# Sums of products copied out of PSUM by ScalarE, and a new order of work, in a state-space layer with a feed-forward layer behind it

## The chip, the cores and the metric

The kernel runs on one core of one Trainium2 chip. The metric is the device time of one execution in microseconds (us), lower is better. A core has five engines that each work through a queue of their own, strictly in order: TensorE (PE in the profile), VectorE (DVE), ScalarE (ACT), GpSimd (POOL) and SyncE (SP), which here only starts transfers. They wait for one another by semaphores.

## What is computed

The input is a sequence of 2048 rows of 512 values. A conditioning vector gives six modulation vectors. The first half normalizes the rows, modulates them, and convolves each of the 512 columns with its own long kernel K (a state-space model, N = 128 states); the second half normalizes again and applies a feed-forward layer of 1792 hidden values with a squared ReLU.

```
P = exp(dt * A * l),  l = 0..L-1                 # complex, 512 x 128 x 2048
K = real(sum over n of C * P * dt*B)             # 512 x 2048
y = irfft(rfft(u padded) * rfft(K padded))[:L] + u * Dskip
x = x + ga * y(layernorm(x) * (1 + ca) + sa)
h = layernorm(x) * (1 + cb) + sb
x = x + gb * (relu(h @ w1 + b1)**2 @ w2 + b2)
```

## The kernel before

The 512 columns are cut into eight groups c of 64, called A to H. The Fourier transforms are matrix products: for each group, "stage 1" (line 714, four pieces) and "stage 2" (line 724, four pieces) transform the input, the same two stages transform K, VectorE multiplies the spectra (line 864), TensorE sums the products back into the time domain (line 872), and the sums are copied from PSUM into the two large tiles `big0` and `big1` (line 878, in `spread`). The inverse transform of line 1040 reads those tiles; the feed-forward layer follows and fills the second half of the time.

K is made in 32 units u of 16 columns, four to a group. Parameters come first, for groups 0 to 3 and then for 4 to 7: products on GpSimd (lines 518, 532 to 539, 570 to 578), rounding and arc tangent on ScalarE (541 to 569) and VectorE (544 to 575). Then ScalarE makes tables of 24 exponentials (line 801; one group with 64 columns or two with 128). For each unit GpSimd adds a phase (line 810) and multiplies table entries (830 and 834), ScalarE takes sine, absolute value and cosine (820, 821, 822), VectorE multiplies (844 to 847), and TensorE multiplies the two halves (854); ScalarE copies the result out (935).

Ahead of the transforms the sixteen row blocks are normalized. VectorE takes statistics (608, 609), GpSimd turns four variances at a time into 1/sqrt by an addition (612) and a power (613), ScalarE scales a selection matrix (672), VectorE scales the row block (670), TensorE makes the transposed, modulated block (674 and 677), and ScalarE copies it out (680). The blocks are counted #0 to #15 below. The rest of the modulation (lines 634, 698 to 705) is `late_modulation`.

All of stage 1, stage 2, line 677, line 872 and the late modulation share three PSUM banks, `ps0` to `ps2`. A bank is written again only when its former content has been copied out. The convolution's K has a bank pair of its own (`kg`), and sine and cosine another (`tg`).

The order in which the program text emits the steps is set by the string ORDER (one field for each unit; r is a row block, A to H a piece of a group's input transform, a to h a piece of its products and sums, x a table of exponentials, l the late modulation, w and digits loads). It sets which bank each step gets and what depends on what. Which instruction each engine runs next is then chosen by `keep_order`: it plays the program through with the durations of `weight` and takes, for each engine, the ready instruction with the longest way to the end; HURRY adds an amount to that length for some steps. Its choice is fixed in the program, so on the chip an engine waits at an instruction that is not ready, with all behind it.

Of the kernel before, what the change touches and what calls it, by code (L numbers as in the profile page):

```python
# [40 lines left out]
EAGER = (0, 0, 0, 0)  # L41
ON_DVE = {}
PACED = 2
HURRY = (147316, 134417, 27026, 378229, -185473, -185396, -357712, -713)
EXPS = [(0, 1), (1, 1), (2, 2), (4, 2), (6, 2)]
ORDER = (
    "rrrrrrrxrrxrrrrrrrCABCBCBCBCAACB.BBCBAAAAlAC...0aaaa1..aDaaa..DbbbbEE.D2D.DEbbD.xbDDb.EccccccE.F"
    ".EEc3c.F.dddd.EdddFF4.dGFF..eGGeeeF.xGG.GeFHHe5Ge..effffGHf.wHf..HH.6ffwwwHg.g.gH.gww7g.gwgwhhhh"
    "g"
).split(".")  # L50


# [37 lines left out]
def free_size(ap):  # L90
    return math.prod(n for _, n in ap.ap[1:])
# [21 lines left out]
def weight(ins):  # L113
# [3 lines left out]
    if "DMA" in type(ins).__name__:  # L117
# [32 lines left out]
        case "Pool":  # L150
            wide = operands(ins.ins)
            whole = bool(wide) and all(a.ap[-1][0] == 1 and len(a.ap) == 2 for a in wide)
            t = 140 + (2.13 if whole else 1.91 if str(wide[0].bass_ap.dtype) == str(I32) else 1.75) * n if wide else 70 + 1.2 * n
        case _:
            t = 30
# [186 lines left out]
def tile_adaln_ssm_ffn(  # L342
# [18 lines left out]
    nc = tc.nc  # L361
# [79 lines left out]
    z4 = [[f[:, 1024 * c : 1024 * c + 1024].rearrange("p (j d) -> p j d", j=64) for c in range(NC)] for f in flat]  # L441
# [160 lines left out]
    for _ in parameters(0, HEAD):  # L602
        pass
    hurry(mark, HURRY[0])

    mark = len(nc.cur_bb.bb.instructions)
    for s in range(16):
        nc.vector.bn_stats(sts[s % 4], rows[s])
        nc.vector.bn_aggr(mv1[:, s, :], sts[s % 4])
        if s % 4 == 3:  # L610
            var = mv1[:, s - 3 : s + 1, 1]
            nc.gpsimd.tensor_scalar(var, var, EPS, None, op0=ALU.add)
            nc.gpsimd.tensor_tensor(var, var, rsq, op=ALU.pow)
    hurry(mark, HURRY[1])

    for c, n in ((HEAD, NC - HEAD),):
        mark = len(nc.cur_bb.bb.instructions)
        decay(4, 4)
        for _ in parameters(c, n):
            pass  # L620
        hurry(mark, HURRY[2])

# [35 lines left out]
    nc.vector.scalar_tensor_tensor(shift, shift.bitcast(F32), second, s4, op0=ALU.mult, op1=ALU.subtract)  # L658
    hurry(mark, HURRY[3])
    spectra.extend(wms[0:3])  # L660
# [197 lines left out]
    def product_pieces(c):  # L858
        xu, sw, xk = xus[c], sws[c], xks[c]
        yr, yu = spectrum(), spectrum()  # L860
        for g in range(4):
            ps = stage2(xk, g)
            for y, x in ((yr, sw), (yu, xu)):
                nc.vector.tensor_mul(product_piece(y, g), ps, piece(x, g))  # L864
            if g == 3:
                spectra.extend((sw, xu, xk))
            yield

        def sums(ps, g, i, js):
            for h, y in ((0, yu), (1, yr)):  # L870
                for m in range(2):
                    nc.tensor.matmul(  # L872
                        ps[64 * m : 64 * m + 64], pairs(y)[:, g, i // 2, 64 * m : 64 * m + 64, i % 2],
                        e1_sb[:, h].rearrange("p (r j) -> p r j", r=2)[:, :, js], start=(h == 0), stop=(h == 1))

        def spread(ps, js, ds):
            for r in range(2):
                nc.vector.tensor_copy(z4[r][c][:, js, ds], ps.rearrange("p d r j -> p j d r")[..., r])  # L878

        j0 = 0  # L880
        if c == NC - 1:
            j0 = 16
            ps = bank("ps", PS).rearrange("p (d r j) -> p d r j", d=16, r=2)
            for d in range(16):
                sums(ps[:, d], d // 4, d % 4, slice(0, j0))
            spread(ps, slice(0, j0), slice(0, 16))
            yield
        for g in range(4):
            ps = bank("ps", PS).rearrange("p (d x) -> p d x", d=4)[:, :, 0 : 128 - 2 * j0]
            ps = ps.rearrange("p d (r j) -> p d r j", r=2)  # L890
            for i in range(4):
                sums(ps[:, i], g, i, slice(j0, 64))
            spread(ps, slice(j0, 64), slice(4 * g, 4 * g + 4))
            if g == 3:
                spectra.extend((yr, yu))
            yield
# [367 lines left out]
```

## Time and profile before

| | |
|---|---|
| median of 3 runs | 633.45 us (632.07 to 634.69) |
| profiled execution | 632.78 us, span 631.0 us |
| TensorE matmul busy | 588.7 us, 93% of the span |
| VectorE busy | 372.3 us, 59% |
| ScalarE busy | 348.5 us, 55% |
| GpSimd busy | 298.1 us, 47% |
| transfers | 42.32 MB, 67 GB/s on average |

The span is the time from the first to the last instruction of the profiled execution; its own time is 1.78 us longer. Shares are averages over stages that differ: up to 62 us the input is loaded and the rows are prepared, from 62 to about 285 us the transforms run, and from about 320 us on the feed-forward layer.

### The profile page before, as it was taken

What the parts mean: (1) busy time and instruction counts of PE and PEld (TensorE: products, weight loads), DVE (VectorE), ACT (ScalarE), POOL (GpSimd) and SP (SyncE); (2) the same over time, 40 slices, a digit from 0 to 9 for tenths busy, and PEclk for the clock granted to TensorE, in tenths of its full rate; (3) what the DMA queues carried; (4) which work ended last, traced back from release to release, by engine and by line L of the source; (5) the groups of instructions that cost most, each with busy time, mean ns of one, the idle gap of its engine ahead of it and who ended that gap; (6) DMA issues with size and microseconds to landing.
All of it is one profiled execution on the core that took longest, in us unless ns stands there. A gap on an engine that the chain in (4) does not pass through costs nothing.

```text
span 631.0 us, 21224 instructions
## 1 busy us (share of the span) xinstructions
PE 588.7 (93%) x9474; PEld 508.2 (81%) x9474; DVE 372.3 (59%) x652; ACT 348.5 (55%) x651; POOL 298.1 (47%) x247
## 2 busy tenths in 40 slices
PE   1488998999999999998999999999999999999996
PEld 1355988899999999897778888888888888888885
DVE  6888779889688998746556332632326332252224
ACT  4937999979969868543757432253323433222220
POOL 6589799999998998148677300010000100000000
PEclk9979999999999999998999999999999999999999
DMA  8940104131221135465244100100001000010001
GB/s 316 395 146 8 63 12 97 36 70 25 49 50 25 37 82 143 125 187 164 87 137 115 36 1 0 68 0 2 0 1 67 1 1 0 1 66 1 0 1 66
DMA packets 23418, 42.32 MB, mean 67 GB/s; under 512 B 4000, under 2 KB 9504, under 8 KB 23200
## 3 DMA queue, kind: packets, MB, share of 16 engines
q1 hardware_dynamic: 22896, 40.84, 22.0%
q8 instruction: 74, 1.21, 0.8%
q10 hardware_dynamic: 432, 0.14, 0.1%
q14 instruction: 16, 0.13, 0.1%
HBM read 28.39 MB, written 4.19 MB: 52 GB/s over the span
## 4 chain that ended last, share of the span: by engine, by line
PE 75%; ACT 9%; POOL 9%; issue 3%; DVE 3%; DMA 0%; DVEq 0%; POOLq 0%
PE tg L1165 8%; PE tg L1167 8%; PE tg L1166 8%; PE ps L872 7%; PE ps L1131 6%; PE ps L1132 6%; PE ps L1134 6%; PE ps L724 5%; PE ps L714 5%; PE kg L854 3%; PE tg L1040 3%; PE kg L1131 2%; PE kg L1132 2%; PE kg L1134 2%; ACT tables L801 2%
## 5 line engine op out<-in xcount | busy, mean ns | idle before, releaser
L1153 DVE SCALAR_TENSOR_TENSOR ps<-ps,b1c,xy 128x512 f32<-128x512 f32 x42 | 31.8, 756 | 110.7 <-ACT xy L1151 110.7
L1151 ACT ACTIVATE xy<-ps,b1c 128x512 f32<-128x512 f32 x42 | 29.0, 690 | 122.6 <-PE ps L1134 122.6
L1076 POOL TENSOR_TENSOR big<-big,lo 128x512 f32<-128x512 f32 x12 | 15.6, 1300 | 146.9 <-DVE xy L1073 146.5
L724 PE MATMUL ps<-xy,t_sb 128*64 128x64 f32 x2048 | 67.7, 223 | 1.7 <-issue 1.7
L724 PEld LDWEIGHTS ps<-xy,t_sb 128*64 128x64 f32 x2048 | 63.8, 138 | 4.6 <-issue 2.1
L872 PE MATMUL ps<-e_sb,xy 128*64 128x128 f32 (+2 forms) x1152 | 63.6, 266 | 1.9 <-ACT xy L716 1.5
L872 PEld LDWEIGHTS ps<-e_sb,xy 128*64 128x64 f32 x1152 | 58.6, 139 | 3.5 <-ACT xy L716 2.0
L716 ACT COPY xy<-ps 128x512 f32<-128x512 f32 x64 | 36.9, 589 | 13.5 <-PE ps L714 13.4
L834 POOL TENSOR_TENSOR rtl<-tables 128x1024 f32<-128x1024 f32 x22 | 43.3, 1970 | 0.2
L864 DVE TENSOR_TENSOR xy<-ps,xy 128x512 f32<-128x512 f32 x64 | 39.2, 680 | 2.4 <-PE ps L724 1.9
L1131 PE MATMUL ps<-h0h,w1h 128*128 128x512 f32 (+1 forms) x96 | 36.1, 382 | 0.0
L810 POOL TENSOR_TENSOR rtl<-lo,big 128x1024 int32<-128x1024 int32 x16 | 34.3, 2143 | 3.5 <-ACT tg L822 2.8
L810 POOL TENSOR_TENSOR llph<-lo,big 128x1024 int32<-128x1024 int32 x16 | 34.5, 2155 | 1.4 <-ACT tg L822 1.4
L714 PE MATMUL ps<-d_sb,ksb 128*64 128x128 f32 x512 | 34.1, 274 | 0.8 <-DVE xy L864 0.7
L878 DVE COPY big<-ps 128x256 f32<-128x256 f32 (+1 forms) x66 | 24.1, 407 | 17.0 <-PE ps L872 16.9
L714 PE MATMUL ps<-d_sb,big 128*64 128x128 f32 x512 | 32.0, 274 | 1.1 <-ACT big L680 0.7
L1131 PE MATMUL ps<-h,w1h 128*128 128x512 f32 x80 | 31.4, 393 | 0.0
L1153 DVE SCALAR_TENSOR_TENSOR kg<-kg,b1c,xy 128x512 f32<-128x512 f32 x14 | 10.6, 758 | 34.8 <-ACT xy L1151 34.8
L1151 ACT ACTIVATE xy<-kg,b1c 128x512 f32<-128x512 f32 x14 | 9.6, 688 | 37.8 <-PE kg L1134 37.8
L714 PEld LDWEIGHTS ps<-d_sb,ksb 128*64 128x64 f32 x512 | 28.3, 137 | 1.8 <-DVE xy L864 0.9
L714 PEld LDWEIGHTS ps<-d_sb,big 128*64 128x64 f32 x512 | 28.0, 137 | 1.9 <-ACT big L680 1.0
L845 DVE TENSOR_TENSOR rtl<-rtl,tg 128x1024 f32<-128x1024 f32 x22 | 26.6, 1211 | 1.1 <-POOL rtl L834 1.1
(287 smaller groups left out, 1608.3 us busy)
## 6 DMA issues: line engine op xcount, KB each, us to landing
xy<-xt SPq DMA_DIRECT2D x32, 256.0 KB, 4.5
xy<-xy SPq DMA_DIRECT2D x32, 256.0 KB, 3.4
xy<-w_mod SPq DMA_DIRECT2D x6, 1024.0 KB, 8.5
out_dram<-xy SPq DMA_DIRECT2D x16, 256.0 KB, 2.1
xy<-w SPq DMA_DIRECT2D x14, 256.0 KB, 2.7
raw<-w SPq DMA_DIRECT2D x6, 512.0 KB, 4.9
t_sb<-c_t SPq DMA_DIRECT2D x1, 2048.0 KB, 11.0
i2c<-c_i SPq DMA_DIRECT2D x4, 512.0 KB, 4.4
```

Source lines behind the costliest of these rows:

```text
L714: nc.tensor.matmul(ps[64 * r : 64 * r + 64, 128 * i : 128 * i + 128], src[:, i], d1_sb[:, r], start=True, stop=True)
L724: nc.tensor.matmul(ps[64 * r : 64 * r + 64, 64 * i : 64 * i + 64].rearrange("p (h q t) -> p q h t", h=2, t=2), t2_sb[:, 8 * g + i, r], src ...
L810: nc.gpsimd.tensor_tensor(ph.rearrange("p d r (a b) -> p (d r) a b", a=4), bc(low_phase[:, us].rearrange("p d r b -> p (d r) b"), 2, 4), b ...
L834: nc.gpsimd.tensor_mul(am[:, 0, :, 32:96].rearrange("p d (v x) -> p d v x", v=2), bc(et[:, 256 + 8 * d0 : 384 + 8 * d0].rearrange("p (y a) ...
L872: nc.tensor.matmul(ps[64 * m : 64 * m + 64], pairs(y)[:, g, i // 2, 64 * m : 64 * m + 64, i % 2], e1_sb[:, h].rearrange("p (r j) -> p r j" ...
L1131: pe.append(nc.tensor.matmul(ps, w1h[:, q, fs], hh[:, q, cols], start=(q == 0), stop=False))
L1132: pe.append(nc.tensor.matmul(ps, wl[:, q], hh[:, q, cols], start=False, stop=False))
L1134: pe.append(nc.tensor.matmul(ps, w1h[:, q, fs], hl[:, q, cols], start=False, stop=(q == 3)))
L1153: nc.vector.scalar_tensor_tensor(ps, ps, b1c[:, t : t + 1], rr, op0=ALU.add, op1=ALU.mult)
L1165: pe.append(nc.tensor.matmul(acc, r2l[:, ms], hi_, start=(f == 0), stop=False))
L1166: pe.append(nc.tensor.matmul(acc, r2h[:, ms], lo_, start=False, stop=False))
L1167: pe.append(nc.tensor.matmul(acc, r2h[:, ms], hi_, start=False, stop=(f == NF - 1)))
```

## The change

Four things are edited.

- `spread` copies the sums of the products by ScalarE instead of VectorE.
- `weight` gives the power of line 613 (a GpSimd operation on 128 x 4 values with two inputs) 1000 ns; by the general formula it had 147.
- HURRY has eight other numbers.
- ORDER is another string.

```
-HURRY = (147316, 134417, 27026, 378229, -185473, -185396, -357712, -713)
+HURRY = (29580, -181455, -278749, 139035, -280562, -261179, 363664, -461)
 ORDER = (
-    "rrrrrrrxrrxrrrrrrrCABCBCBCBCAACB.BBCBAAAAlAC...0aaaa1..aDaaa..
...
+    "rrrrrrrrrrrrrrrrClABCBCBCCBBAxACB.ABCA.BAAA..C0aaaaa..D.1xaa.a
...
         case "Pool":
             wide = operands(ins.ins)
             whole = bool(wide) and all(a.ap[-1][0] == 1 and len(a.ap) == 2 for a in wide)
+            if len(wide) > 1 and free_size(wide[0]) == 4:
+                return 1000, 1065
...
         def spread(ps, js, ds):
             for r in range(2):
-                nc.vector.tensor_copy(z4[r][c][:, js, ds], ps.rearrange("p d r j -> p j d r")[..., r])
+                nc.scalar.copy(z4[r][c][:, js, ds], ps.rearrange("p d r j -> p j d r")[..., r])
```

Behind line 154 the lines of the changed kernel are two higher (line 613 is its line 615). The order on TensorE from the first matrix product of the inverse transform on is the same in both. Ahead of it, three places matter for what follows. The trailing numbers of names belong to the built program.

The first place is GpSimd's queue from the last parameter product of groups 0 to 3 on (`mv` are the row statistics, `lo` the phases, `tables_379` and `tables_380` the two tables of exponentials, `rtl` and `llph` the tiles of the units). Before:

```order
L572 TENSOR_TENSOR big_83<-big_83 128x4x64
L612 TENSOR_SCALAR mv_71<-mv_71 128x4
L574 TENSOR_TENSOR big_83<-big_83 128x4x128 x3
L613 TENSOR_TENSOR mv_71<-mv_71,small 128x4
L532 TENSOR_TENSOR big_83<-big_83 128x4x64
L533 TENSOR_TENSOR big_83<-big_83 128x4x64
```

The same place now:

```order
L574 TENSOR_TENSOR big_83<-big_83 128x4x64
L806 TENSOR_TENSOR tables_380<-tables_380,big_83 128x64x4 x2
L576 TENSOR_TENSOR big_83<-big_83 128x4x128 x3
L788 TENSOR_TENSOR lo<-lo,big_83 128x128x2 x3
L812 TENSOR_TENSOR rtl<-lo,big_83 128x1024
L806 TENSOR_TENSOR tables_379<-tables_379,big_83 128x64x4
L836 TENSOR_TENSOR rtl<-tables_379 128x16x64
L812 TENSOR_TENSOR llph<-lo,big_83 128x1024
L836 TENSOR_TENSOR rtl<-tables_379 128x16x64
L836 TENSOR_TENSOR llph<-tables_379 128x16x64
L614 TENSOR_SCALAR mv_71<-mv_71 128x4
L615 TENSOR_TENSOR mv_71<-mv_71,small 128x4
```

The power of the last four row blocks, and behind it the parameter products of groups 4 to 7 (now from line 534 on), moved behind the phases and table products of the first units.

The second place is ScalarE's queue among the sixteen row blocks; a copy of line 680 frees the bank of one row block. Before, behind the fifth copy:

```order
L680 COPY big_84<-ps_159 128x128x4
L672 ACTIVATE big_83<-ident,mv_71 128x2x64
L541 ACTIVATE big_83<-big_83,magic 128x4x64
L542 ACTIVATE big_83<-big_83,magic 128x4x64
L550 ACTIVATE big_83<-big_83 128x4x64
L551 ACTIVATE big_83<-big_83 128x4x64
L543 ACTIVATE big_83<-big_83,unmagic 128x4x64
L680 COPY big_84<-ps_157 128x128x4
```

Now, behind the fourth copy (line 682 is the copy, line 822 the first sine):

```order
L682 COPY big_84<-ps_158 128x128x4
L674 ACTIVATE big_83<-ident,mv_71 128x2x64
L822 ACTIVATE tg_425<-rtl 128x1024
L823 ACTIVATE rtl<-rtl 128x1024
L682 COPY big_84<-ps_159 128x128x4
L682 COPY big_84<-ps_157 128x128x4
```

And now, further on, with the copies of #11 to #15 (here with buffer numbers):

```order
L674 ACTIVATE big0_83<-ident_63,mv1_71 128x2x64 x2
L682 COPY big1_84<-ps0_157 128x128x4
L674 ACTIVATE big0_83<-ident_63,mv1_71 128x2x64 x2
L682 COPY big1_84<-ps1_158 128x128x4
L682 COPY big1_84<-ps2_159 128x128x4
L543 ACTIVATE big0_83<-big0_83,magic_64 128x4x64
L544 ACTIVATE big0_83<-big0_83,magic_64 128x4x64
L552 ACTIVATE big0_83<-big0_83 128x4x64
L553 ACTIVATE big0_83<-big0_83 128x4x64
L682 COPY big1_84<-ps0_157 128x128x4
L545 ACTIVATE big0_83<-big0_83,unmagic_65 128x4x64
L682 COPY big1_84<-ps1_158 128x128x4
```

The five parameter steps of groups 4 to 7 moved from between #4 and #5 to between #13 and #15, and the first unit's sine moved ahead of the copy of #4.

The third place is ScalarE's queue at the exponentials of groups 4 and 5 (lines 801, now 803). Before:

```order
L822 ACTIVATE tg1_426<-llph_382,halfpi_67 128x1024
L801 ACT_TABLE_LOAD
L801 ACTIVATE tables0_379<-big0_83 128x2x64 x24
L716 COPY xy0_91<-ps1_158 128x512
L716 COPY xy0_91<-ps0_157 128x512
L935 COPY ksb0_988<-kg0_362 128x256
L820 ACT_TABLE_LOAD
```

And now:

```order
L824 ACTIVATE tg1_426<-llph_382,halfpi_67 128x1024
L803 ACT_TABLE_LOAD
L803 ACTIVATE tables0_379<-big0_83 128x2x64 x24
L880 COPY big0_83<-ps0_157 128x64x4
L718 COPY xy4_95<-ps2_159 128x512
L880 COPY big1_84<-ps0_157 128x64x4
L937 COPY ksb0_1037<-kg0_362 128x256
L718 COPY xy4_95<-ps1_158 128x512
L822 ACT_TABLE_LOAD
```

The exponentials stand at the same place, behind the eighth unit's cosine; what waits behind them now includes a copy of sums (line 880). In all ScalarE loads a table of functions nine times instead of eight, since the exponentials of group 1 now stand between arc tangent and sine.

More of the change, by code (lines that the diff above doesn't have):

```diff
@@ L43 @@
 PACED = 2
-HURRY = (147316, 134417, 27026, 378229, -185473, -185396, -357712, -713)
+HURRY = (29580, -181455, -278749, 139035, -280562, -261179, 363664, -461)
 EXPS = [(0, 1), (1, 1), (2, 2), (4, 2), (6, 2)]
 ORDER = (
-    "rrrrrrrxrrxrrrrrrrCABCBCBCBCAACB.BBCBAAAAlAC...0aaaa1..aDaaa..DbbbbEE.D2D.DEbbD.xbDDb.EccccccE.F"
-    ".EEc3c.F.dddd.EdddFF4.dGFF..eGGeeeF.xGG.GeFHHe5Ge..effffGHf.wHf..HH.6ffwwwHg.g.gH.gww7g.gwgwhhhh"
-    "g"
+    "rrrrrrrrrrrrrrrrClABCBCBCCBBAxACB.ABCA.BAAA..C0aaaaa..D.1xaa.abbbbDEE.D2DbxDDD.EDb..bbccccEccc.F"
+    "..cE3FEE.ddddd.FdFE.G.ddFF4.eeeGxeGF.GFeG.GHH5e.G.eeHffwff.GHH6.HfwffH.H.f..gg.gggwg.www7ghhgwwh"
+    "h"
 ).split(".")
@@ L152, in weight @@
             whole = bool(wide) and all(a.ap[-1][0] == 1 and len(a.ap) == 2 for a in wide)
+            if len(wide) > 1 and free_size(wide[0]) == 4:
+                return 1000, 1065
             t = 140 + (2.13 if whole else 1.91 if str(wide[0].bass_ap.dtype) == str(I32) else 1.75) * n if wide else 70 + 1.2 * n
@@ L877, in spread @@
             for r in range(2):
-                nc.vector.tensor_copy(z4[r][c][:, js, ds], ps.rearrange("p d r j -> p j d r")[..., r])
+                nc.scalar.copy(z4[r][c][:, js, ds], ps.rearrange("p d r j -> p j d r")[..., r])
         j0 = 0
```

## The prediction

> **What bounds the kernel now.** I read the table by stage first, then the waits of TensorE in each stage, then the timeline where a wait is not "issue". The table by stage, from the columns start:end, length and the busy time of each engine:
>
> ```profile
> 20.00:62.00 42.00, 29.20 (x568) 20.44 (x569) 36.25 (x61) 29.70 (x87) 32.67 (x34) 0.88 0.47 165
> 62.00:160.00 98.00, 94.74 (x2746) 89.12 (x2748) 83.39 (x133) 90.68 (x160) 92.20 (x73) 1.00 0.23 54
> 160.00:285.00 125.00, 122.92 (x3575) 116.85 (x3572) 97.78 (x166) 90.63 (x132) 96.29 (x68) 1.00 0.35 88
> 285.00:320.00 35.00, 31.79 (x1116) 26.38 (x1099) 22.45 (x62) 19.91 (x42) 27.67 (x20) 0.95 0.39 117
> ```
>
> The first busy number is TensorE: from 62 to 285 us it is idle for 3.3 + 2.1 = 5.4 us of 223. The fourth is ScalarE, the fifth GpSimd: from 62 to 160 both are full, 90.7 and 92.2 of 98. So the transforms are bound by TensorE, and what can be won there is its idle time; ahead of 62 us other engines decide. Its waits, from the stages 0:62 and 62:160:
>
> ```profile
> PE ps L674 <- ACT big L680: 2.1, 1, 2.1
> PE ps L872 <- ACT xy L716: 1.5, 1, 1.5
> PE ps L714 <- ACT big L680: 0.7, 1, 0.7
> PE ps L714 <- DVE xy L864: 0.7, 1, 0.7
> PE ps L714 <- ACT xy L716: 0.4, 1, 0.4
> ```
>
> These five, 5.4 us, are the waits on work that the change moves. The feed-forward order on TensorE is the same in both kernels, and I count it at nothing.
>
> **The row blocks.** The 2.1 us are this:
>
> ```profile
> 40.89 1.04 POOL L613 TENSOR_TENSOR mv<-mv,small 128x4 f32<-128x4 f32 x1
> 47.18 0.51 ACT L541 ACTIVATE big<-big,magic 128x256 f32<-128x256 f32 x1 [3.00 <-POOL big L538]
> 49.01 1.05 ACT L680 COPY big<-ps 128x512 f32<-128x512 f32 x2
> 49.63 0.50 PE L674 MATMUL ps<-shift,pick 128*128 128x512 f32 x1 [2.08 <-ACT big L680]
> ```
>
> The power takes 1.04 us, the planner gave it 0.15. ScalarE stood at line 541 for a parameter product of GpSimd, the copies behind it came late, and block #8 had no bank. The change prices the power and moves line 541 behind the copy of #13. This wait goes.
>
> What is late next is the first sine (line 820), now ahead of the copy of #4. It needs the phase of line 810 from GpSimd. GpSimd's rows there:
>
> ```profile
> 32.54 0.73 POOL L578 TENSOR_TENSOR big<-big 128x256 int32<-128x256 int32 x1 [3.33 <-ACT big L568]
> 35.60 0.85 POOL L572 TENSOR_TENSOR big<-big 128x256 f32<-128x256 f32 x1
> 36.82 4.10 POOL L574 TENSOR_TENSOR big<-big 128x512 int32<-128x512 int32 x3
> 47.91 2.66 POOL L786 TENSOR_TENSOR lo<-lo,big 128x256 int32<-128x256 int32 x3
> 50.65 2.14 POOL L810 TENSOR_TENSOR rtl<-lo,big 128x1024 int32<-128x1024 int32 x1
> 57.91 2.14 POOL L834 TENSOR_TENSOR rtl<-tables 128x1024 f32<-128x1024 f32 x1
> 61.98 2.21 POOL L804 TENSOR_TENSOR tables<-tables,big 128x256 f32<-128x256 f32 x3
> ```
>
> When does that queue start? ScalarE's early work is shuffled: exponentials of groups 2 and 3 first, group 1 between arc tangent and sine, with one more table load.
>
> ```profile
> 9.41 3.67 ACT L801 ACTIVATE tables<-big 128x64 f32<-128x64 f32 x24 [0.84 <-POOL big L518]
> 13.79 1.28 ACT L672 ACTIVATE big<-ident,mv 128x128 f32<-128x128 f32 x4 [0.71 <-POOL mv L613]
> 18.47 9.12 ACT L801 ACTIVATE tables<-big 128x64 f32<-128x64 f32 x48
> 27.82 1.28 ACT L558 ACT_TABLE_LOAD   x1
> ```
>
> The wide 24 take 9.12 - 3.67 = 5.45, so they end at 14.8; five parameter steps to 16.9, group 0 to 20.5, the arc tangent's part with its load to 23.3, four selections (1.28) to 24.6, load 1.28 and group 1 to 29.5. The cast of line 657, which began at 29.4, stands there now: no gain, no loss, and the first block starts on TensorE at 34.3 as before. Then the sine's load; line 568 ends at 31.8 instead of 32.5, so GpSimd begins 0.7 earlier, and line 572 ends at 35.7.
>
> From there: two table products (2/3 of 2.21 = 1.5), 4.1, 2.7 and 2.1 put the phase at 46.0. ScalarE has been at the sine since 42.8. It runs lines 820 and 821 (1.0 each) and copies #4 at 48.0 to 48.5; block #7, whose bank that is, could have started at 46.0. Wait: 2.4 us in place of the 2.1 removed.
>
> The last power now has 0.8 + 2.0 + 2.2 + 2.1 + 2.0 more ahead of it on GpSimd and ends at 56.4; ScalarE's selection for block #12 waits for it, with the copy of #11 behind: 0.5 us for TensorE. The products of groups 4 to 7 start only then; before they took from 41.9 to 48.0, so they end at 62.4. Line 551 needs the last of them, and the copies of #14 and #15 stand behind it. Rows of before at this place:
>
> ```profile
> 61.36 0.58 ACT L680 COPY big<-ps 128x512 f32<-128x512 f32 x1 [0.85 <-PE ps L677]
> 62.00 1.20 PE L714 MATMUL ps<-d_sb,big 128*64 128x128 f32 x18 [0.70 <-ACT big L680]
> 67.61 0.73 POOL L570 TENSOR_TENSOR big<-big 128x256 f32<-128x256 f32 x1 [3.42 <-ACT big L567]
> ```
>
> TensorE ends #15 at 62.2, about 0.9 later than before. Its next step, a late modulation, takes the bank of #14, copied at 63.4: wait 1.2. The first line 714 starts at 64.5, 2.5 us later than before, with 1.05 us of modulation done: 1.5 behind. The transposes of the modulation then wait for VectorE, which has the reciprocal of line 555 ahead of the copy of line 698; by the rows of those steps 0.3 and 0.9. Subtracting the old 0.4, I take 2.3 behind at 85 us. SyncE's third late modulation load goes to a tile whose readers end at 42 us, not 61, so it lands in time and costs nothing.
>
> The bounds: the chain of GpSimd is plain addition, and I see no way to less than 1 us of it; if VectorE shares its time badly with GpSimd, as in its rows of 2 us there, 4 us.
>
> **The exponentials of groups 4 and 5.** The same GpSimd delay reaches them. GpSimd stopped at line 570 for line 567; the new chain (line 551 at 62.8, reciprocal, arc tangent, sine) gives 70.4 instead of 67.6. It is full from there to 100 us, so the eighth unit's cosine and the table load behind it slide from 104.0 to about 106.4.
>
> ```profile
> 103.99 1.28 ACT L801 ACT_TABLE_LOAD   x1
> 105.29 5.75 ACT L801 ACTIVATE tables<-big 128x128 f32<-128x128 f32 x24
> 110.81 1.14 ACT L716 COPY xy<-ps 128x512 f32<-128x512 f32 x2
> 111.52 3.72 PE L872 MATMUL ps<-e_sb,xy 128*64 128x128 f32 x64 [1.51 <-ACT xy L716]
> ```
>
> Before, line 872 waited for the first copy behind the exponentials. Now it waits for the second, since a copy of sums stands ahead: 106.4 + 1.3 + 5.5 + 0.3 + 0.5 = 114.0 against 111.5. At that point TensorE has run the same steps in both kernels (18 of line 714, 16 of 724, 7 of 854, the late modulation). So the change is 2.5 us behind, the row blocks' loss included: the two are one term, not two.
>
> **From there to the end.** Of what stands behind, line 820's load keeps one copy 0.2 us late. At the exponentials of groups 6 and 7 TensorE had 7.4 us of work that VectorE drains or that needs no bank, and did not wait; now 0.87 + 1.75 + 1.75 = 4.4 stand between the unit's product and a bank that ScalarE must free. I take 0.5, with bounds 0 and 3.5.
>
> ```profile
> 208.73 1.08 PE ps L724 x32
> 211.56 1.05 PE kg L854 x64
> 215.57 1.75 PE ps L872 x32
> 217.32 0.87 PE ps L714 x16
> ```
>
> **The copies.** 66 leave VectorE.
>
> ```profile
> L878 DVE COPY big<-ps 128x256 f32<-128x256 f32 x58 | 21.6, 415 | 13.0 <-PE ps L872 13.0
> 75.32 0.37 ACT L935 COPY ksb<-kg 128x256 f32<-128x256 f32 x1
> 75.58 0.60 ACT L748 COPY xy<-ps 128x512 f32<-128x512 f32 x1
> ```
>
> No ScalarE copy of sums is in the trace. The nearest row is line 935, also 256 values out of PSUM, which holds ScalarE for 0.26 us (75.32 to 75.58); the far end is VectorE's 0.41. That is 17 to 27 us more on ScalarE; I take 0.27 each, 18 us. Nearly all of it falls behind 114 us; from 160 to 285 ScalarE is idle 34 us, which covers it on average. What is queued behind a waiting ScalarE are the copies of lines 716 and 748, so TensorE pays when a pair of copies stands behind 1 us of sine or cosine with all three banks full. I take 0.3 us for the whole; the bounds are -0.7 (VectorE, relieved, no longer holds up line 714) and +8 (a quarter us at each of the 33 pairs).
>
> **The sum.** 2.5 + 0.2 + 0.5 + 0.3 = 3.5 us. The profiled execution of 632.78 becomes 636.3; the median of the runs lies 0.67 above it, so 637.0.
>
> **The rule on table loads.** In this trace a switch costs its 1.28 us and no more: the cosine before the load above ends at 103.98 (102.86 + 1.12), the load starts at 103.99, the first exponential at 105.29.
>
> ```profile
> 102.86 1.12 ACT L822 ACTIVATE tg<-llph,halfpi 128x1024 f32<-128x1024 f32 x1
> ```
>
> [...]
>
> **The rivals.**
>
> - *The delay is absorbed, no change.* GpSimd catches up between 85 and 106 us, and the exponentials come as early as before. For it: only the cosine's time, not TensorE's own delay, sets 114.0. Against: GpSimd's full queue. It leaves the 0.2 + 0.5 + 0.3 of what comes behind, 634.5.
> - *Faster, the sine is not waited for.* It is decided by GpSimd's chain between line 572 and the first phase: 10.4 us by the rows; at 7.2 the sine is ready when ScalarE reaches it, the new wait of 2.4 is gone and with it most of what follows. Then the old waits 2.1 + 0.7 + 0.4 + 1.5 + 0.7 go for little in return: 5.4 less 1.4 is 4, time 629.5. Against it: every row of that chain is longer than the planner's formula, a table product 0.74 against 0.59.
> - *ScalarE becomes the bound.* Its queue is nine tenths full behind 114 us, and each pair of copies delays a bank by a quarter us: 8 us, time 641.5. It decides if ScalarE's idle share between 110 and 260 us falls under a twentieth. Against it: 34 idle us for some 16 of copies.
> - *A switch costs twice its load.* If ScalarE also stood still for one more load's 1.28 us, the added switch ahead of the cast of line 657 would delay the first block by that: 638.3. Against it: the 0.01 us between the cosine and the load at 103.99.
>
> **How the numbers follow.** A run of this kernel tells 0.5%, 3.2 us, from no change. Forecast 0.49 (its own range 634.8 to 639: the row blocks at 1 to 4 us in place of 2.5, with the end of 0.7 below nothing for the copies at the low side and half a us at the high one), absorbed 0.26, faster 0.14, ScalarE 0.08, the dearer switch 0.03. The forecast of 3.5 lies at that bound, and I split it 0.29 slower and 0.20 same. Slower: 0.29 + 0.08 + 0.03 = 0.40; same: 0.20 + 0.26 = 0.46; faster 0.14. The range of 8 in 10 leaves out most of the faster case and the far half of the ScalarE case: 631.0 to 641.0.
>
> **What would show it.** In the changed profile: ScalarE waits for line 812 (the phase) for about 3 us near 46, and TensorE for the copy of line 682 near 48; ScalarE waits for line 541's product near 62; the table load of line 803 stands at 106; line 874 waits about 3 us near 114. I am wrong if the load stands before 104, if the wait near 46 is under 1 us, or if TensorE's waits on ScalarE behind 120 us add up to over 3 us.

## The result, and the profile after

The changed kernel takes 637.72 us (median of 11 runs, 635.26 to 642.86), the kernel before 635.18 in the runs taken with it (11, 632.07 to 639.17). The ratio is 1.0050, with a 95% interval of 1.0026 to 1.0074: 3.2 us slower, 1.6 to 4.7. The forecast was 3.5 us slower. The profiled execution took 635.77 us with a span of 634.0, against 632.78 and 631.0 before. Where medians and ratios of a run differ in what follows, the ratio counts, since it leaves disturbed runs out.

The same four stages as before, with the same columns (TensorE first, VectorE third, ScalarE fourth, GpSimd fifth, then the granted clock):

```profile
20.00:62.00 42.00, 29.39 (x568) 20.76 (x568) 29.09 (x53) 28.39 (x78) 34.85 (x37) 1.00 0.55 191
62.00:160.00 98.00, 91.39 (x2660) 85.08 (x2662) 76.56 (x118) 91.59 (x166) 87.32 (x69) 1.00 0.18 39
160.00:285.00 125.00, 121.73 (x3492) 115.92 (x3492) 87.61 (x127) 105.18 (x186) 96.56 (x67) 1.00 0.33 82
285.00:320.00 35.00, 31.74 (x1078) 27.43 (x1075) 18.32 (x50) 21.05 (x48) 27.29 (x19) 1.00 0.47 136
```

TensorE lost 3.4 us of work from 62 to 160 (91.39 against 94.74) and 1.2 from 160 to 285. ScalarE took over the copies: 105.18 instead of 90.63 from 160 to 285, VectorE 87.61 instead of 97.78. TensorE's waits from 36 to 100 us, and from 100 to 290:

```profile
PE ps L676 <- ACT big L682: 1.5, 1, 1.5
PE ps L636 <- ACT big L682: 1.4, 1, 1.4
PE ps L716 <- DVE cbc L703: 0.9, 1, 0.9
PE ps L636 <- ACT xy L718: 0.4, 1, 0.4
...
PE ps L874 <- ACT xy L718: 1.7, 2, 1.0
PE ps L874 <- DVE xy L866: 1.6, 3, 0.7
PE ps L726 <- DVE xy L866: 1.4, 2, 1.2
PE kg L856 <- DVE ksb L938: 0.8, 1, 0.8
```

None of them is a wait for a copy of sums (line 880). The timeline at the places that the prediction named, by engine:

```profile
33.51 0.94 DVE L577 TENSOR_SCALAR big<-big 128x512 int32<-128x512 int32 x1 [1.14 <-POOL big L576]
34.52 0.71 DVE L672 SCALAR_TENSOR_TENSOR xy<-xy,mv,kg 128x512 f32<-128x512 f32 x1
...
35.38 1.94 PE L679 MATMUL ps<-xy,big 128*32 128x128 f32 x32 [4.10 <-DVE xy L672]
48.42 0.50 PE L676 MATMUL ps<-shift,pick 128*128 128x512 f32 x1 [1.49 <-ACT big L682]
63.13 1.08 PE L636 MATMUL ps<-xy,srep 128*32 128x128 f32 x32 [1.42 <-ACT big L682]
...
43.61 2.14 POOL L812 TENSOR_TENSOR rtl<-lo,big 128x1024 int32<-128x1024 int32 x1
70.47 0.72 POOL L572 TENSOR_TENSOR big<-big 128x256 f32<-128x256 f32 x1 [7.84 <-DVE big L577]
...
24.73 1.28 ACT L803 ACT_TABLE_LOAD   x1
45.78 1.03 ACT L822 ACTIVATE tg<-rtl 128x1024 f32<-128x1024 int32 x1 [2.21 <-POOL rtl L812]
55.86 0.69 ACT L674 ACTIVATE big<-ident,mv 128x128 f32<-128x128 f32 x2 [0.95 <-POOL mv L615]
61.08 0.51 ACT L543 ACTIVATE big<-big,magic 128x256 f32<-128x256 f32 x1 [1.59 <-POOL big L540]
107.00 1.28 ACT L803 ACT_TABLE_LOAD   x1
108.30 5.75 ACT L803 ACTIVATE tables<-big 128x128 f32<-128x128 f32 x24
113.86 0.40 ACT L880 COPY big<-ps 128x256 f32<-128x256 f32 x1
114.17 0.57 ACT L718 COPY xy<-ps 128x512 f32<-128x512 f32 x1
...
114.79 1.97 PE L874 MATMUL ps<-e_sb,xy 128*64 128x128 f32 x32 [0.74 <-ACT xy L718]
```

The chain is the one that was walked: ScalarE at the sine waits for the phase, TensorE behind it for a copy; the selection waits for the power; line 543 waits for GpSimd's products, and the late modulation for the copy behind it. The chain of work that ended last, followed back in the trace, goes the same way: GpSimd's queue alone from 31.9 to 61.1 us, through the phase, the power and the products of groups 4 to 7, then line 543, the copy behind it, the late modulation, lines 569 and 572, a cosine at 76.47, then ScalarE's queue alone up to the exponentials, their copies and line 874 at 114.79. So line 874 starts 3.3 us later than its counterpart before (111.52).

The next table is worked out from the traces, since two orders can't be laid side by side row by row. At each moment of a kernel I add up the matrix products that TensorE has done, each at its usual duration, and look up when the kernel before had done as much. The difference, in us, is how far the kernel is behind (minus: ahead). It is good to about half a us.

| us from the start | 44 | 60 | 85 | 105 | 120 | 150 | 190 | 240 | 270 | 340 |
|---|---|---|---|---|---|---|---|---|---|---|
| changed kernel | 0.8 | 0.4 | 2.3 | 2.2 | 3.2 | 3.1 | 3.4 | 3.7 | 3.1 | 3.2 |
| spread_on_vector | 1.8 | 0.4 | 2.3 | 2.3 | 3.3 | 3.9 | 4.5 | 5.6 | 5.0 | 7.2 |
| spread_on_scalar | 1.3 | 0.5 | 0.5 | 1.3 | 0.6 | 1.1 | 4.6 | 4.8 | 4.8 | 6.1 |
| copies_moved_alone | 0.2 | 1.4 | 1.4 | 1.2 | 1.8 | 3.8 | 4.8 | 6.0 | 7.1 | 10.9 |
| copies_back_alone | 2.3 | 1.0 | 2.9 | 2.8 | 3.8 | 4.5 | 3.7 | 6.5 | 6.2 | 10.8 |
| hurry_only | -0.5 | 2.9 | 7.4 | 7.5 | 9.9 | 11.5 | 12.9 | 15.4 | 16.0 | 18.7 |
| order_only | 0.0 | 0.0 | 6.3 | 5.5 | 10.4 | 11.8 | 13.4 | 13.9 | 13.8 | 14.4 |
| gpsimd_early | 0.6 | 0.1 | 1.9 | 2.3 | 2.7 | 3.2 | 3.0 | 3.2 | 3.2 | 6.1 |
| three_moves | 2.3 | 0.0 | 2.2 | 2.3 | 3.3 | 3.2 | 3.5 | 3.9 | 4.3 | 5.3 |
| row_blocks_again | -0.2 | -2.4 | 0.1 | -0.2 | -0.1 | 0.1 | -0.8 | -0.9 | -1.1 | -0.3 |

In the changed kernel all is lost by 120 us: 2.3 us up to 85, about 1 more at the exponentials. Between 270 and 340 us most of the other kernels lose more. All but order_only (granted 1.00 from 285 to 325 us) have a stretch of half clock about there, and the profiled run of the changed kernel has none (1.00); the last section comes back to it. The kernel before has one too (0.50 from 294.9 to 298.3 us), which may make the changed kernel look a little better behind it.

### The profile page after: what moved, and what is told of

The parts are those of the page before. It is cut to its first block, busy times and chain, and to the rows that moved or that the text cites. A ratio compares the mean times of both kernels' runs of the same rounds, so it can differ in the third digit from the quotient of the medians.

```text
span 634.0 us, 21243 instructions
## 1 busy us (share of the span) xinstructions
PE 587.5 (93%) x9474; PEld 507.3 (80%) x9474; DVE 345.9 (55%) x586; ACT 366.9 (58%) x718; POOL 297.0 (47%) x247
## 4 chain that ended last, share of the span: by engine, by line
PE 66%; ACT 16%; POOL 6%; DMA 4%; issue 4%; DVE 3%; DVEq 0%; ACTq 0%; POOLq 0%; SPq 0%
PE tg L1167 8%; PE tg L1169 8%; PE tg L1168 8%; PE ps L1133 6%; PE ps L1134 6%; PE ps L1136 6%; PE ps L726 4%; PE ps L716 4%; PE ps L874 4%; ACT tables L803 3%; PE kg L856 2%; ACT tg L824 2%; ACT tg L822 2%; PE kg L1133 2%; PE kg L1134 2%
## 5 line engine op out<-in xcount | busy, mean ns | idle before, releaser
L874 PE MATMUL ps<-e_sb,xy 128*64 128x128 f32 (+2 forms) x1152 | 63.4, 266 | 3.5 <-ACT xy L718 1.7
L718 ACT COPY xy<-ps 128x512 f32<-128x512 f32 x64 | 38.4, 610 | 11.4 <-PE ps L716 9.4
L812 POOL TENSOR_TENSOR rtl<-lo,big 128x1024 int32<-128x1024 int32 x16 | 34.3, 2142 | 3.6 <-ACT tg L824 3.0
L812 POOL TENSOR_TENSOR llph<-lo,big 128x1024 int32<-128x1024 int32 x16 | 34.3, 2143 | 0.3 <-ACT tg L824 0.3
L1089 ACT ACTIVATE ps<-ps,sbc,cbc 128x128 f32<-128x128 f32 x44 | 18.9, 430 | 14.8 <-PE ps L1082 13.8
```

The source lines that it names most:

```text
L812: nc.gpsimd.tensor_tensor(ph.rearrange("p d r (a b) -> p (d r) a b", a=4), bc(low_phase[:, us].rearrange("p d r b -> p (d r) b"), 2, 4), b ...
L874: nc.tensor.matmul(ps[64 * m : 64 * m + 64], pairs(y)[:, g, i // 2, 64 * m : 64 * m + 64, i % 2], e1_sb[:, h].rearrange("p (r j) -> p r j" ...
```

## The experiments

### The copies alone, and the rest alone, planned anew

One line each. The planner is left to find its order again; up to some 97 us (kernel before) or 85 us (changed kernel) it finds the old one.

```
 spread_on_vector (from the changed kernel)
-                nc.scalar.copy(z4[r][c][:, js, ds], ...
+                nc.vector.tensor_copy(z4[r][c][:, js, ds], ...
 spread_on_scalar (from the kernel before)
-                nc.vector.tensor_copy(z4[r][c][:, js, ds], ...
+                nc.scalar.copy(z4[r][c][:, js, ds], ...
```

> The changed kernel with the copies of the sums back on VectorE; ORDER, HURRY and the power's price stay new, and every engine's queue up to about 90 us stays as it is. Theory A, the row blocks and parameters: TensorE is about 2.2 us behind the kernel before at 85 us, as in the changed kernel, and the whole stays 2 to 4 us slower than before. Rival B, the copies on ScalarE cost the time: not more than 1 us slower than before.

Measured: 639.71 us against 634.39, ratio 1.0077 (1.0047 to 1.0107). At 85 us it is 2.3 us behind, the same as the changed kernel, and at 120 us 3.3 (3.2): the loss up to there, which is all of the changed kernel's, has nothing to do with the copies. Theory A holds there, rival B falls. But the whole is 4.9 us slower than before, beyond the 2 to 4: with VectorE copying, 2.3 us are lost from 120 to 240 us, in the changed kernel 0.5.

> The kernel before with nothing changed but the copies of the sums, now on ScalarE; the queues up to about 65 us stay as they were. Theory A: nothing is lost up to 85 us and the whole lies within 1 us of before. Rival B: 2.5 to 4 us slower than before, lost behind 105 us, where the copies begin.

Measured: 638.52 us, ratio 1.0056 (1.0029 to 1.0082), 3.6 us slower. Theory A is wrong on this one: nothing is lost up to 85 us, as it said, but behind 150 us 3.5 us are, and those are rival B's. The copies on ScalarE are not free in the old order. So both halves are dear, 4.9 and 3.6 us, and both together cost 3.2: they don't add.

### HURRY alone and ORDER alone

The kernel before with HURRY or ORDER from the change, nothing else.

> The kernel before with the new HURRY alone: GpSimd has the last power and the products of groups 4 to 7 behind the first phases, as in the changed kernel, while the late modulation stays where it was. Theory A: TensorE waits for copies behind line 541 near 61 us and is 0.7 to 1.5 us behind at 70 us; the whole is 1 to 2 us slower than before. Rival C, only the place of the late modulation among the first transforms costs: nothing is lost by 70 us, the whole within 0.5 us of before.

> The kernel before with the new ORDER alone: the row blocks' queues stay as before up to 61 us, and the late modulation comes among the first transforms. Theory A: nothing lost up to 62 us, then the waits of the late modulation, 0.4 and 0.9 us, less the 0.7 and 0.4 that the kernel before waits there; the whole 0 to 1.5 us slower. Rival C: the full 2.2 us are lost between 62 and 85 us.

Measured: 648.79 us, ratio 1.0224 (1.0188 to 1.0259), and 649.31 us, ratio 1.0220 (1.0182 to 1.0258). 14 us each: all theories miss by far. The waits of TensorE in hurry_only from 36 to 75 us:

```profile
PE ps L677 <- ACT big L672: 4.3, 1, 4.3
PE ps L714 <- ACT big L680: 3.0, 1, 3.0
```

The two longest of order_only from 62 to 120 us:

```profile
PE ps L724 <- DVE xy L864: 3.7, 1, 3.7
PE ps L714 <- DVE mt L698: 1.6, 1, 1.6
```

In hurry_only the selections wait for a power that GpSimd has behind the first phases and that the plan still has at its old price (the change prices it); in order_only TensorE waits for VectorE's products. In both kernels a stretch at half the clock comes with these waits (granted clock 0.50 from 55.6 to 62.4 us, 0.51 from 66.2 to 73.1), which takes up to 3.4 us more, half of its length. This covers most of the 7.4 us that hurry_only has lost by 85 and of the 10.4 that order_only has lost by 120; the rest, up to 15.4 and 13.9 at 240, was not followed. That the old price is what makes hurry_only so slow was not tried. ORDER, HURRY and the power's price are one setting: a part of it, put into the other kernel, says nothing of what that part does in the whole, and these two runs tell the theories apart in nothing.

### The copies moved, everything else pinned

To measure the copies without a new plan, the planner is told that they run on the old engine, and they are put into the new engine's queue at the times planned for them. What every engine does otherwise, and in which order, stays.

```
+def planned(ins):
+    return "DVE" if ins.name in spreads else ...      # copies_back_alone: "Activation"
...
-        eng = str(ins.engine).split(".")[-1]
+        eng = planned(ins)
...
+    for v in last.values():
+        v.sort(key=lambda x: x[0])                     # by planned start
```

> The kernel before with the copies of the sums on ScalarE and the order of everything else on every engine as it was: the copies are planned as VectorE's and put into ScalarE's queue at the times planned for them. Theory F, a copy that stands behind the exponentials or a sine in ScalarE's queue frees its bank late: 2.5 to 4.5 us lost between 105 and 175 us, in waits of line 872 and 714 for ScalarE. Rival G, the 3.6 us that the kernel before lost with the copies on ScalarE and its queues planned anew came from the other work that moved: under 1 us lost, as the prediction had it (0.3).

Measured: 642.58 us against 634.62, ratio 1.0122 (1.0072 to 1.0172), 7.7 us. Theory F holds in kind: 3.6 us are lost from 105 to 190, and the waits go on behind that, which it had not. The last 3.8 us, from 270 to 340, come with half clock (6.8 us from 309 on) and are no wait for a copy. The two longest of TensorE's waits from 100 to 290 us (line 887 is the copy of sums here, 723 and 725 stage 1 and its copy):

```profile
PE ps L723 <- ACT big L887: 4.9, 5, 1.6
PE ps L881 <- ACT xy L725: 2.1, 3, 1.4
```

And the timeline where it is worst:

```profile
158.92 5.81 ACT L810 ACTIVATE tables<-big 128x128 f32<-128x128 f32 x24
164.52 0.70 ACT L887 COPY big<-ps 128x256 f32<-128x256 f32 x2
...
165.27 1.09 PE L723 MATMUL ps<-d_sb,ksb 128*64 128x128 f32 x16 [0.80 <-ACT big L887]
...
167.56 1.03 ACT L829 ACTIVATE tg<-rtl 128x1024 f32<-128x1024 int32 x1
168.52 0.37 ACT L887 COPY big<-ps 128x256 f32<-128x256 f32 x1
...
168.94 1.09 PE L723 MATMUL ps<-d_sb,big 128*64 128x128 f32 x16 [1.53 <-ACT big L887]
```

A pair of copies of a third of a us each stands behind 5.8 us of exponentials, and one behind a load and a sine; the bank comes free when they are done. It is not the copy's length that costs, but what stands ahead of it in its queue.

> The changed kernel with the copies of the sums on VectorE and the order of everything else on every engine as the change has it (planned as ScalarE's, put into VectorE's queue at the times planned for them). Theory F, a copy costs TensorE only where it stands behind exponentials or a sine, and the new order leaves it no such place: no wait of TensorE for a copy of sums either way, the whole within 1.5 us of the changed kernel. Rival H, the new order only hides a loss that the copies on ScalarE still bring: 2.5 us or more faster than the changed kernel, level with the kernel before.

Measured: 642.98 us against 633.72, ratio 1.0162 (1.0132 to 1.0191), where the changed kernel had 1.0050. Both theories are wrong: taking the copies off ScalarE again makes the changed kernel 5 us slower by the medians, 7 by the ratios. Two of the waits of TensorE from 100 to 290 us (line 889 is the copy, now VectorE's):

```profile
PE ps L725 <- DVE big L889: 2.2, 2, 1.4
PE ps L735 <- DVE big L889: 0.9, 3, 0.5
```

These waits, 3.1 us, are what it loses on the changed kernel up to 270 us. The other 4.6, from 270 to 340, come with 3.4 us of half clock and with waits of line 1051 (the inverse transform) for which the profile names no cause, 5.3 us against 2.0 in the changed kernel; what they have to do with the copies is not shown. So the copies belong to the order that was found with them: there TensorE never waits for one. In an order found for the other engine the whole is 5 to 8 us slower either way. When the order is planned anew, 3.6 and 4.9 us remain against the kernel before.

### Moves in the front, all else pinned

For the next six the order that the planner chose is kept on every engine, and single instructions are moved behind others: `MOVES` holds the engine, what is moved, and behind what.

gpsimd_early, from the changed kernel (amp1, amp2 are the second and third unit's table products of line 836, par.9 the last product of groups 4 to 7):

```
+MOVES = (
+    ("Pool", ["amp1.1", "amp2.1"], "par.9"),
```

> The changed kernel with every engine's order fixed as it chose it, but for GpSimd: the table products of the second and third unit go behind the last power and the products of groups 4 to 7, which so come 3.7 us earlier. Theory A: the power is done by 52 us, line 543 no longer waits for GpSimd near 61 us, TensorE's wait of 1.4 us for the copy of block #14 shrinks to 0.2, and TensorE is 1.2 to 1.6 us less behind at 85 us than in the changed kernel; the whole gains 1 to 1.5 us on it. Rival D, the exponentials near 107 us decide alone: the gain at 85 us is lost again by 120 us and the whole is within 0.5 us of the changed kernel.

Measured: 638.68 us against 634.62, ratio 1.0075 (1.0045 to 1.0105), not faster than the changed kernel. The power was done at 52 us and the wait for copy #14 is gone, as expected: the first product of the transforms starts at 62.24, 1.9 us ahead of the changed kernel (64.14). But nearly the same wait stands one step on, and the transpose behind it starts at 65.08 against 65.17. At 85 us the kernel is 0.4 us less behind, at 105 no more. The timeline of VectorE and TensorE (line 873 is the sine's product of the second unit, 726 the late modulation's copy, 728 the transpose behind it):

```profile
59.94 1.22 DVE L873 TENSOR_TENSOR rtl<-rtl,tg 128x1024 f32<-128x1024 f32 x1 [7.51 <-POOL rtl L862]
...
63.12 1.75 DVE L575 RECIPROCAL big<-big 128x256 f32<-128x256 f32 x1
64.79 0.23 DVE L726 COPY mt<-ps 128x128 f32<-128x128 f32 x1
...
65.08 0.33 PE L728 MATMUL ps<-ident,mt 128*128 128x128 f32 x1 [1.75 <-DVE mt L726]
```

VectorE waits 7.5 us for the table product that was put off, and the reciprocal stands behind it at 63.1 as it did in the changed kernel. I had looked at GpSimd and ScalarE and not at what VectorE's queue has ahead. Neither theory A's size nor rival D's place is right.

sine_later, from the changed kernel (sin0 is the first unit's sine and absolute value, r5.19 the copy of #5):

```
+    ("Activation", ["sin0.0", "sin0.1"], "r5.19"),
```

> The changed kernel with its order fixed, but for ScalarE: the first unit's sine and absolute value go behind the copies of blocks #4 and #5. Theory A: the wait of 1.5 us at 48 us is gone, but the power of the last four blocks is still done only at 55.6 us, so TensorE waits 1.5 to 1.7 us for the selection of block #12 instead of 0.2; at 60 us nothing is gained, and the whole is within 0.5 us of the changed kernel. Rival E, the waits of the row blocks add up one by one: 1.5 us gained at 60 us.

Measured: 639.16 us, ratio 1.0075 (1.0045 to 1.0106). In its trace the wait for copy #4 is gone and this one, from 44 to 64 us, stands in its place:

```profile
PE ps L704 <- ACT big L699: 1.0, 1, 1.0
```

That is the selection that waits for the power, as theory A has it; and the whole is not faster than the changed kernel, as rival E's 1.5 us would have made it. (By 31 us this execution was already 1.5 us behind at half the clock, granted 0.57 on average from 20 to 36 us, so its place at 60 us says nothing more.)

three_moves, both of these together with two more:

```
+    ("Pool", ["amp1.1", "amp2.1"], "par.9"),
+    ("Activation", ["sin0.0", "sin0.1"], "r5.19"),
+    ("Activation", ["sin1.0"], "r9.19"),
+    ("Activation", ["sin1.1"], "r11.19"),
+    ("DVE", ["par0.42"], "r0.0"),
```

> The changed kernel with its order fixed, but for both of these moves together, the second unit's sine behind the copies of #9 and #11, and on VectorE the first row block ahead of the shift of line 577 that waits for GpSimd. Theory A: the first block starts 1 us earlier, the waits at 48, 56 and 63 us are gone or under 0.3 us each, and at 85 us TensorE is 3 to 4 us ahead of the changed kernel (1 to 1.7 ahead of before); the whole is 3 to 4 us faster than the changed kernel and level with the kernel before or up to 1 us faster. Rival D: what is gained is lost at the exponentials near 107 us, at least 2 us of it.

Measured: 641.05 us, ratio 1.0111 (1.0070 to 1.0153): slower than the changed kernel, if anything. The waits at 48, 56 and 63 us are gone, and the blocks are level with the kernel before at 60 us (the 2.3 us at 44 in the table come with slow products: the 32 of a block, line 708, take 1.93 to 1.94 us up to 41.9 us in this run and 1.08 from 44.4 on, in the changed kernel 1.08 from 40.1 on); then, from 44 to 100 us, TensorE waits

```profile
PE ps L732 <- DVE mt L730: 2.1, 1, 2.1
```

for the same copy of VectorE (line 730 here). The gain was gone by 72 us, long ahead of rival D's exponentials.

four_moves (without the last move, and VectorE takes the second unit's products later; par.39 is the shift of line 577 for groups 4 to 7):

```
-    ("DVE", ["par0.42"], "r0.0"),
+    ("DVE", ["rl1.0", "rl1.1"], "par.39"),
```

> As the run with three moves, but the first row block stays where it was and VectorE takes the products of the second unit's sine behind the arc tangent's part of the parameters, so that nothing there waits for GpSimd's late table product ahead of the late modulation's copy. Theory A with the row-block waits one behind the other: the wait of 2.1 us for that copy is gone, TensorE is 1.5 to 2.5 us less behind at 85 us than in the changed kernel, and the whole gains 1 to 2.5 us on it. Rival D, the exponentials near 107 us: what is gained is lost by 120 us.

Measured: 639.90 us against 633.72, ratio 1.0124 (1.0093 to 1.0156). The wait was to go, and it grew. VectorE and TensorE:

```profile
59.97 1.94 DVE L570 TENSOR_SCALAR big<-big 128x256 int32<-128x256 f32 x1
61.83 2.17 DVE L576 SCALAR_TENSOR_TENSOR big<-big 128x256 f32<-128x256 f32 x1
...
65.98 0.33 PE L732 MATMUL ps<-ident,mt 128*128 128x128 f32 x1 [2.95 <-DVE mt L730]
```

The same two steps in the changed kernel:

```profile
62.17 0.62 DVE L548 TENSOR_SCALAR big<-big 128x256 int32<-128x256 f32 x1
62.71 0.41 DVE L554 SCALAR_TENSOR_TENSOR big<-big 128x256 f32<-128x256 f32 x1
```

Now they run while GpSimd computes the two table products that were put off, and take 1.9 and 2.2 us instead of 0.6 and 0.4: what GpSimd gained, VectorE paid. The whole is not faster than the changed kernel, so neither theory A's gain nor rival D's loss of it came.

before_row_blocks, from the kernel before: the parameter steps of line 541 on behind the copies of #7 and #8, the first sine behind #13.

```
+    ("Activation", ["par.10", "par.11"], "r7.19"),
+    ("Activation", ["par.17", "par.18", "par.12"], "r8.19"),
+    ("Activation", ["sin0.0", "sin0.1"], "r13.19"),
```

> The kernel before with its order fixed, but for ScalarE: the five parameter steps of line 541 on stand behind the copies of #7 and #8, and the first sine behind the copy of #13. Theory A: the wait of 2.1 us for the copy of #5 is gone, and TensorE is 1.5 to 2.1 us ahead of the kernel before at 64 us. By the prediction's reading of line 872 (its wait ends with ScalarE's exponentials, not with TensorE's own work) the gain is lost at 112 us, where the wait grows from 1.5 to 3 us or more, unless the exponentials come earlier too; the whole within 0.7 us of before. Rival J, the waits add: 2 us faster than before.

Measured: 636.93 us, ratio 1.0013 (0.9974 to 1.0052). TensorE ends the row blocks 1.9 us ahead, then waits 2.8 us for the copies of the last two blocks, which stand behind the moved sine. That is 2.1 us more than the kernel before waits there, and the gain is spent: the first line 714 starts at 62.11, before at 62.00. (This execution took 639.88 us, with half clock in three stretches behind 60 us: 0.51 from 63.4 to 66.8, 0.52 from 302 to 309, 0.57 from 326 to 330; so nothing is read from its end.)

row_blocks_again takes the sine and two signs out of that place too:

```
+    ("Activation", ["par.24", "par.26"], "r15.19"),
-    ("Activation", ["sin0.0", "sin0.1"], "r13.19"),
+    ("Activation", ["sin0.0"], "A0-19.8"),       # behind the second copy of line 716
+    ("Activation", ["sin0.1"], "C0-21.8"),       # behind the fourth
```

> The kernel before with its order fixed, but for ScalarE: the five parameter steps of line 541 on behind the copies of #7 and #8, the two signs of lines 557 and 559 behind the copy of #15, and the first sine and absolute value among the copies of the first transforms, so that no copy of a row block stands behind a step that waits. Theory A: no wait of TensorE over 0.4 us between 36 and 62 us, the first line 714 starts at 59.8 to 60.3 us (62.0 before), no stretch of half clock between 60 and 70 us, and TensorE is 1.5 to 2.1 us ahead of before at 85 us. By the prediction's reading of line 872 (its wait ends with ScalarE's exponentials) the gain is lost at 112 us, where the wait grows from 1.5 to over 3 us, and the whole is within 0.7 us of before. Rival J, the gain stays: 1.5 to 2.1 us faster than before, a version faster than both kernels.

Measured: 633.24 us against 634.41, ratio 0.9985 (0.9956 to 1.0014): no difference that the runs tell. The first line 714 starts at 59.58, a little ahead of what theory A said, 2.4 us ahead of before. TensorE's waits from 36 to 100 us (lines 744 and 746 are stage 1 and its copy):

```profile
PE ps L744 <- ACT xy L746: 2.0, 4, 0.6
PE ps L744 <- ACT big L709: 0.7, 1, 0.7
```

The 2.4 us are given back between 62 and 72 us, at the copies that now share ScalarE with the sine, and not at 112 us, where I looked for it: there line 872 waits 1.4 us as before. ScalarE is full there (busy for 92.0 of the 98 us from 62 to 160 in this run), so what is moved out of the front delays what stands behind it. This is the best of the versions run, and not shown to be faster than the kernel before.

## Why the prediction was right

The time came out as forecast, and so did the cause of the larger part of it, the late queue of GpSimd in the front. That the sum is as near as 3.5 to 3.2 is in part luck: the loss up to the exponentials was 0.7 us larger than forecast, and the 1.0 us of small terms behind them (0.2, 0.5 and 0.3) did not come. Nor did the prediction stake much on the sign: it gave slower 0.40 and same 0.46. The single steps, in its order:

- *The first sine.* Phase done at 46.0 by the working, 45.75 in the trace; ScalarE waited 2.2 us, not about 3, and TensorE 1.5, not 2.4, because the first block began at 35.4, not at 34.3. That step was mis-sized: VectorE's shift of line 577 waits 1.1 us for GpSimd ahead of the first row block. It cost nothing, because the phase ends the wait at the same 48.4 either way.
- *The power* was done at 55.8 (forecast 56.4) and cost TensorE 0.2 us (0.5).
- *The products of groups 4 to 7* ended at 61.85 (62.4); the wait behind line 543 was 1.4 us (1.2), the two of the late modulation 0.4 and 0.9 (0.3 and 0.9; but only the second is for VectorE, the first is for ScalarE's copy of line 718), line 572 began at 70.47 (70.4). At 85 us the kernel is 2.3 us behind (2.3). That this loss belongs to the order and not to the copies is shown: with the copies back on VectorE it is the same 2.3, with the copies alone on ScalarE 0.5, the error of the table; and the first copy starts only at 113.9.
- *The exponentials of groups 4 and 5.* The load stands at 107.0 (106.4), line 874 behind them at 114.79 (114.0), so the path is the one that was named. But its last part is not GpSimd's: from 76.5 to 107 us ScalarE never waits for GpSimd and is full by itself (busy for 30.4 of the 30.5 us). And the sign that was given, a wait of line 874 of about 3 us, is not there: it waits 0.7. On the way TensorE had already waited for VectorE (0.8, 0.2, 0.6 and 0.7 us between 105 and 112), so that its own work ended only 0.7 us ahead of the copy; earlier exponentials alone would have given no more than that there. The later exponentials, near 160 us, gave and took: 5 us behind at 170, 3.4 at 190.
- *The copies.* 21.5 us on ScalarE for 66 (384 ns of duration each, forecast 17 to 27), and in the changed kernel no wait of TensorE for one: 0.3 us was near. But the reason that I gave, idle time that covers them on average, is wrong, and the small size was luck: the working did not follow where the new order puts the copies in ScalarE's queue. Moved alone they cost 7.7 us, near the far end of 8. The condition of the rival that ScalarE becomes the bound was nearly met: its idle share from 110 to 260 us fell from 18% to 7.5%, and the rival asked for less than 5%. The other sign, waits of TensorE on ScalarE behind 120 us of over 3 us, needs care: up to 290 us they are 1.0, to the end of the kernel 3.2, of which 2.2 stand in the inverse transform and the feed-forward layer, where the kernel before has 1.0 and where the table shows nothing lost.
- *The table load.* The added one starts at 24.73, right behind the selections (23.46 + 1.26 = 24.72), and the first exponential at 26.02. The one near 107 us stands right behind the cosine again (105.86 + 1.12 = 106.98, load at 107.00). So the rival of a dearer switch had nothing for it.
- *The range.* The low end of the forecast's own range was summed wrongly: with 1 us for the row blocks and -0.7 in place of the 0.3 for the copies it is 634.5, not 634.8. Nothing rests on it.

What was not settled: the sum of the parts. Copies and order are 3.6 and 4.9 us when each is planned anew, and 3.2 together, so there is no share of the 3.2 that is the copies' alone: the loss was there before the first copy, but what copies and order did to each other behind 120 us was not taken apart. And none of the six kernels with moves in the front, each aimed at a wait that the trace shows of TensorE, was measurably faster than the kernel it came from: I have shown where each gain went up to 72 us, not a version without the loss.

## What to carry to other kernels

A wait that the trace names was not worth its length here where the engine that ends it had no slack behind it: row_blocks_again won 2.4 us in the front and had given them back by 72 us, with ScalarE busy for 92.0 of the 98 us from 62 on. Where two or three engines are over nine tenths full (from 62 to 160 us before: TensorE 94.74, GpSimd 92.20 and ScalarE 90.68 of 98 us), follow each one's queue past the wait (all of them, VectorE's too) before counting the gain. The price of moving the copies to ScalarE was what stood ahead of them in its queue, not their duration (7.7 us for 66 copies of 380 ns, moved alone), so it can't be measured apart from the order: measure both with the order pinned, and with it planned anew. Half of a jointly searched setting is no experiment on that half.

## What the runs showed of the hardware that I had not expected

The clock. The prediction treats TensorE's clock as full. In the changed kernel's profiled run it is (granted 1.00), from 39 us, where its record begins, to 633 us. In the others it falls to a half in places, for 3.4 us or a multiple of it (the kernel before: 10.2 us from 28.6 on and 3.4 from 294.9 on; up to 20.5 us, sine_later from 22.1 on), and in twelve of thirteen where the inverse transforms begin (between 294 and 312 us). gpsimd_early, the third column from the end being the granted clock:

```profile
298.40:301.80 3.40, 2.05 (x85) 1.40 (x84) 3.26 (x12) 2.27 (x6) 1.41 (x2) 1.00 0.61 161
301.80:312.10 10.30, 9.65 (x200) 7.76 (x200) 3.96 (x10) 6.91 (x16) 3.92 (x4) 0.50 0.35 104
```

The changed kernel at the same place:

```profile
298.40:301.80 3.40, 2.49 (x87) 1.82 (x88) 3.05 (x9) 2.32 (x8) 2.55 (x2) 1.00 0.72 177
301.80:312.10 10.30, 8.46 (x302) 7.03 (x298) 5.51 (x17) 8.90 (x20) 4.74 (x4) 1.00 0.33 99
```

200 matrix products instead of 302 in the same time: from 270 to 340 us gpsimd_early goes from 3.2 to 6.1 us behind, and the changed kernel from 3.1 to 3.2. So one execution's end can lie 3 us from another's with the same order on TensorE, and a gain of that size in one trace is none. The clock goes with a part of the spread of times: the kernel before was run in four series of 17 to 23 executions, 7 to 10 us from the fastest to the slowest, and in three of them a lower mean clock goes with a longer time (correlations of -0.56, -0.67 and -0.80, where -1 would be a straight line); in the fourth there is none (-0.04). By the means it is not what makes the changed kernel slower: 0.989 over its eleven executions, 0.986 to 0.989 for the kernel before in these series.

TensorE was not idle ahead of gpsimd_early's fall at 301.8 us: it was busy for 2.05 of the 3.4 us. In all fourteen traces the clock falls 21 times between 40 us and the last 10 us, and in the 3.4 us ahead TensorE was busy for 0.81 (order_only, from 107.2 on) to 2.35 us (the kernel before, from 291.5 on, mostly with products of 32 rows and 32 columns). It was as little busy elsewhere without a fall behind it (1.72 us, gpsimd_early, from 63.4 on, at 1.00 there and in the 3.4 us behind), so what decides is not shown.

The second is the pair VectorE and GpSimd, of which the prediction had only rows of 2 us and a bound: the steps that take 0.41 and 0.62 us in the changed kernel take 2.17 and 1.94 in four_moves, beside GpSimd products. There GpSimd's products start first, at 59.61 and 61.72, for 2.15 and 2.00 us, and VectorE's steps end 0.15 and 0.28 us after them. The changed kernel's step of 0.62 us also ends 0.15 us after a shorter product that GpSimd began first (line 806, 0.83 us from 61.81 on). The traces show these times, not what is behind them.
